# One left residual on ScalarE's DMA queue, and the third segment's main rows stored straight from SBUF

## The chip, the cores and the metric

The kernel runs on one core of a Trainium2 chip. The metric is the device time of one execution in microseconds (us), as a median of several runs. Before the change it is 1885.16 us (three runs, 1883.83 to 1887.8). The profiled execution has a span of 1876.8 us, at a mean granted TensorE clock of 0.993.

## What is computed

The result is `x + A(xn) + B(xn)` for one sequence of 2048 tokens of 1024 features, with `xn` the layer norm of `x`. B is a two-layer feed-forward net with a GELU. A is a recurrence over 64 segments of 32 tokens, each with 8 memory rows in front:

```python
def _A_ref(x, mem0, Wq, Wk, Wv, Wo, seg_len):
    ...
    mem = mem0
    for s in range(n_seg):                       # 64 segments of 32 tokens
        h = jnp.concatenate([mem, xs], axis=1)   # 8 memory rows and 32 tokens
        q = jnp.einsum('btd,dhe->bhte', h, Wq)   # k, v likewise; 32 heads of 128
        ...
        o = jnp.einsum('bhte,hed->btd', o, Wo)
        mem = o[:, :M, :].copy()                 # the next segment's memory
        outs.append(o[:, M:, :])

x = A_x
xn = _layernorm(x, axis=-1)
return x + _A_ref(xn, A_mem0, ...) + _B_ref(xn, B_w1, B_b1, B_w2, B_b2)
```

All tensors are bf16. A segment needs the memory rows of the one before, so the 64 segments run one after the other.

## The kernel before, in words

**First stage (to about 435 us).** Layer norm and the feed-forward net. `R_n` in DRAM gets `x + B(xn)`, the residual that A's rows are added to. `turn_R` (L426) copies its rows in DRAM into `hr_d` and `hrL_d`, where a later load finds them in the layout that the attention's output has. For the last 16 segments (the last four calls of `turn_R`) these copies aren't issued at once: they are put on a list, `small`, in segments s = 1 to 4 (L686), 13 or so in a segment, and are issued on GpSimd's queue one or two at a time, whenever a streamed weight unit is done (L672 to L674).

**Second stage: one pass per segment, for s = 0 to 63.** The weights Q, K, V and O are cut into 64 units of 128 x 2048 elements (512 KB), in the order K0, Q0, K1, Q1, V0, V1 (8 units each), O (16 units). 46 units stay in SBUF, 18 are streamed in each segment: two of these are copied from PSUM by VectorE, and the other 16 are loaded from DRAM on SyncE's queue into six rotating buffers. `start_stream` (L243) issues the next load in program order, when the unit that sat in the buffer has been used by TensorE.

Each segment's tokens are split. Its first 24 tokens and the 8 memory rows are the **main** rows, done in the segment itself. The last 8 tokens of four neighbouring segments are the **left** rows, done together as a group of 32 rows: `i4 = s % 4` says where in its group a segment is. Left rows go through O in segments with i4 = 1 (`left_o`), which therefore have two residuals to add: `st["res"]` for the main rows, in `res_home` (the right half of `hr_home`), and `st["resL"]` for the left rows, in `pr_all` (the last 256 columns of `half_home`). `pr_all` also holds the exponentials of the scores (L820), so `resL` can be loaded only when VectorE has read the last of them in this segment (L860), and the next segment's exponentials can be written only when the left rows have been stored.

**At the end of a segment**, in program order:

1. L975 loads the next segment's rows into `hr_home` (`load_x_rows`, L263): on ScalarE's queue for s < 5, on GpSimd's from s = 5 on. From s = 5 on that load brings the residual as well, so it overwrites `res_home` and must wait until the stores from it have landed. For s < 5 the residual comes by a load of its own on ScalarE's queue (L968, `load_res`).
2. In the loop over the O units (L992), `load_res` comes after unit 0, `resL` (L1000, i4 = 1) after unit 1, and in segments with i4 = 3 the closure `rows_of_main` after unit 2.
3. ScalarE casts the memory rows (L1005), TensorE multiplies them into place (L286) and VectorE copies them into the next segment's input (L290). Only then can the next segment's K0 pass begin.
4. VectorE adds the residuals to the accumulator in PSUM (L1020), `resL` first. The accumulator is one of three banks that rotate through all passes, and is free only after that.
5. The rows are stored. With i4 = 1 they go to a DRAM buffer `outL_d` by four stores (L1025) and from there to the output (L1050, by way of `small`). With i4 = 0 or 3, four stores of 24 x 512 bytes go from SBUF to the output (L1058). With i4 = 2, one store of 128 x 512 bytes goes to the DRAM buffer `outM_d` (L1052), and in the next segment SyncE copies it from there to the output, DRAM to DRAM (L1055).

Everything an engine does or issues is in one order, the program's. A wait on GpSimd's queue holds up all that stands behind it there.

Of the kernel before, what the change touches and what calls it, by code (L numbers as in the profile page):

```python
# [10 lines left out]
BF16 = mybir.dt.bfloat16  # L11
# [6 lines left out]
P = 128  # L18
# [19 lines left out]
NX = 24  # L38
NL = SEG - NX
GRP = 4  # L40
NGRP = NSEG // GRP
# [45 lines left out]
def kernel(  # L87
# [16 lines left out]
    nc = tc.nc  # L104
# [3 lines left out]
    out_flat = out.rearrange("b s d -> (b s) d")  # L108
# [10 lines left out]
    dram = ctx.enter_context(tc.tile_pool(name="dram", bufs=1, space=bass.MemoryType.DRAM))  # L119
# [3 lines left out]
    hrL_d = dram.tile([NGRP + 1, P, 512], BF16, name="hrL_d")  # L123
    R_n = dram.tile([S, DM], BF16, name="R_n")
    outL_d = dram.tile([NGRP, 2 * SEG, DM], BF16, name="outL_d")
    outM_d = dram.tile([NGRP, P, 256], BF16, name="outM_d")


    place = nc.lookup_mloc("DynamicDMAScratchLoc")
# [22 lines left out]
    def slab(place):  # L152
        if place in low:
            return low[place]
        return slabs.tile([P, 2048], BF16, name="u", tag=place)
# [10 lines left out]
    for j in range(4):  # L166
# [11 lines left out]
        out=m, in_=m, pattern=[[1, NX]], compare_op=ALU.is_ge, fill=0.0, base=0, channel_multiplier=-1,  # L178
    )
    for half in range(2):  # L180
        m = mask_left[0:SEG, :, 8 - 8 * half:16 - 8 * half]
        nc.gpsimd.affine_select(
            out=m, in_=m, pattern=[[-8, GRP], [0, 8]], compare_op=ALU.is_ge, fill=0.0, base=0, channel_multiplier=1,
        )
        nc.gpsimd.affine_select(
            out=m, in_=m, pattern=[[8, GRP], [1 if half else 0, 8]], compare_op=ALU.is_ge, fill=0.0,
# [110 lines left out]
    with tc.tile_pool(name="ma", bufs=2) as ma, tc.tile_pool(name="mps", bufs=6, space=PSUM) as mps:  # L297
# [35 lines left out]
        for j in range(4):  # L333
            nc.sync.dma_start(
                out=o_sb[32 * j + NX:32 * j + 32, 0:8, :],
                in_=mem0[:, 256 * j:256 * j + 256].rearrange("m (h e) -> m h e", h=8),
# [4 lines left out]
        for i in range(14):  # L341
            t = slab(f"w2_{i}")[:, :].rearrange("p (c d) -> p c d", d=DM)
# [146 lines left out]
        for tg in range(4):  # L489
# [14 lines left out]
            for fb in range(FC):  # L504
                ps = mps.tile([P, 512], F32, name="ps")
                for kt in range(KT):
# [9 lines left out]
                    out=xb[:, :], in_=ps[:, :], func=ACT.Identity, bias=b1col[:, fb:fb + 1], scale=1.0  # L516
# [4 lines left out]
                    out=u[:, :], in0=u[:, :], scalar1=0.044715, scalar2=1.0, op0=ALU.mult, op1=ALU.add  # L521
# [94 lines left out]
    with tc.tile_pool(name="late", bufs=1) as late, \  # L616
# [10 lines left out]
        def new_acc():  # L627
            bank = free_banks.popleft()
            ps = banks.tile([P, 512], F32, name="acc", tag=bank)
            bank_of[id(ps)] = bank, ps  # L630
            return ps
# [20 lines left out]
        def unit_tile(unit):  # L652
            nonlocal used
            if IS_STREAMED[unit]:
                used += 1
                return stream_tiles.pop(used - 1)[:, :]
            return res_tiles[unit]
# [8 lines left out]
        def unit_done(unit):  # L666

            if IS_STREAMED[unit]:
                start_stream(slot_of.pop(used - 1))
                if late_units:  # L670
                    fetch_late(late_units.popleft())
                for _ in range(2 if len(small) > 8 else 1):  # L672
                    if small:
                        small.popleft()()  # L674
# [7 lines left out]
        for s in range(NSEG):  # L682
            g, i4 = divmod(s, GRP)
# [12 lines left out]
            og, slot = divmod(s + 2, GRP)  # L696
            m0 = main_row(slot)
            st = {}
# [81 lines left out]
            def q_left(u):  # L780

                if i4 >= 2 + u and more:
                    q = qS[:, i4 - 2 - u, :, :]
                else:
                    q = qL[u][:, :, NL * i4:NL * i4 + NL]
                nc.vector.tensor_copy(out=q_home[:, :, 0:NL], in_=q)
# [13 lines left out]
            def scores(u, meanwhile=None):  # L800

                kT, qL_ends = st["kT", u], ends(q_home)
                sA = mixed[:, 0:160].rearrange("p (c q) -> p c q", q=40)
                sB = mixed[:, 160:224].rearrange("p (c q) -> p c q", q=16)
                for c in range(4):
                    for j in range(4):
                        q = slice(32 * j, 32 * j + 32)
                        nc.tensor.matmul(  # L808
                            sA[q, c, :], lhsT=kT[:, 4 * c + j, :], rhs=q_home[:, 4 * c + j, :],
                            start=(c == 0), stop=True, skip_group_check=True, tile_position=(0, 32 * j),  # L810
                        )
                    for j in range(4):
                        q = slice(32 * j, 32 * j + 32)
                        nc.tensor.matmul(  # L814
                            sB[q, c, :].rearrange("p (a b) -> p a b", b=NL), lhsT=kL[u][:, 4 * c + j, :],
                            rhs=qL_ends[:, 4 * c + j, :, :],
                            start=False, stop=True, skip_group_check=True, tile_position=(0, 32 * j),
                        )
                pr = pr_all[:, 0:224]
                nc.scalar.activation(out=pr, in_=mixed[:, 0:224], func=ACT.Exp, scale=INV_SQRT_DH)  # L820
                prA = pr[:, 0:160].rearrange("p (c q) -> p c q", q=40)
                prB = pr[:, 160:224].rearrange("p (c q) -> p c q", q=16)
                if meanwhile is not None:
                    meanwhile()
                for p, m in ((prA[:, :, NL:SEG], mask_order), (prB, mask_left[:, i4, :])):
                    n = m.shape[-1]
                    nc.vector.tensor_tensor(out=p, in0=p, in1=m[:, None, :].to_broadcast([P, 4, n]), op=ALU.min)
                st["pr", u] = prA, prB
# [94 lines left out]
            at = {} if first else {1: [lambda: q_left(0)]}  # L923
# [7 lines left out]
            if left_q[0] and not first:  # L931
# [4 lines left out]
            at = {  # L936
                0: [lambda: scores(0, None if first else lambda: q_left(1)), lambda: nc.vector.transpose(out=nat_home, in_=nat_home)],
                6: [lambda: sums(0)],
            }
# [19 lines left out]
            at = {0: [lambda: scores(1)], 4: [lambda: sums(1)]}  # L959
# [22 lines left out]
            if left_v[1]:  # L982
                at = {4: [lambda: values(1, (0,))], 6: [lambda: values(1, (1,))]}
            else:
                at = {5: [lambda: values(1, (0, 1))]}
            if left_v[1] and not first:
                at[9] = [lambda: left_values(1, psV1L)]
            at.setdefault(0, []).append(load_res)
            if i4 == 3:
                at.setdefault(2, []).append(rows_of_main)  # L990
            psX = new_acc()
            for n, unit in enumerate(O_UNITS):  # L992
                t = unit_tile(unit)
                o_product(unit, t, psX)
                unit_done(unit)
                for fn in at.get(n, ()):
                    fn()
                if n == 1 and left_o:
                    st["resL"] = pr_all
                    nc.gpsimd.dma_start(out=st["resL"][:, :], in_=hrL_d[og, :, 256:512])  # L1000
            nw = 2 if left_o else 1
            if not final:
                o_sb = nat_home
# [13 lines left out]
            res, rows = st["res"], slice(s * SEG, s * SEG + NX)  # L1017
# [13 lines left out]
            if final:  # L1031
                engines = [nc.sync, nc.scalar, nc.gpsimd]
                n = 0
                for w, r in enumerate(tiles):
                    for b in range(2):
                        cs = slice(256 * (2 * b + w), 256 * (2 * b + w) + 256)
                        pieces = [(rows, slice(64 * b + m0, 64 * b + m0 + NX))]
                        for sl, row in left_rows:
                            p0 = 64 * b + NL * sl
                            pieces.append((slice(row, row + NL), slice(p0, p0 + NL)))  # L1040
                        for o, i in pieces:
                            engines[n % 3].dma_start(out=out_flat[o, cs], in_=r[i, :])
                            n += 1
            elif left_o:
                pairs = [(out_flat[rows, :], outL_d[og, m0:m0 + NX, :])]
                pairs += [
                    (out_flat[row:row + NL, :], outL_d[og, NL * sl:NL * sl + NL, :]) for sl, row in left_rows
                ]
                for o, r in pairs:
                    small.append(lambda o=o, r=r: nc.gpsimd.dma_start(out=o, in_=r))  # L1050
            elif i4 == 2:
                nc.gpsimd.dma_start(out=outM_d[g, :, :], in_=res[:, :])  # L1052
                o = out_flat[rows, :].rearrange("t (j c) -> j t c", j=4)
                r = outM_d[g, :, :].rearrange("(j t) c -> j t c", j=4)[:, 0:NX, :]
                rows_of_main = lambda o=o, r=r: nc.sync.dma_start(out=o, in_=r)  # L1055
            else:
                for j in range(4):
                    nc.gpsimd.dma_start(out=out_flat[rows, 256 * j:256 * j + 256], in_=res[32 * j:32 * j + NX, :])  # L1058
# [37 lines left out]
```

## Time and profile before

| what | value |
|---|---|
| median of 3 runs | 1885.16 us |
| span of the profiled execution | 1876.8 us |
| TensorE busy | 1724.5 us (92%) |
| VectorE, ScalarE, GpSimd busy | 903.2, 650.0, 233.3 us |
| DMA | 614.17 MB, mean 327 GB/s |
| first segment's L1005 | at 458.6 us |
| last segment's L1005 (s = 62) | at 1848.0 us |

A segment is measured here from one L1005 (the cast of its memory rows) to the next. By that measure the 62 segments s = 1 to 62 take 22.4 us each on average. In a view by windows, "PEclk" is the granted share of TensorE's clock, and "DMA share" the time that packets took, as a share of the 16 DMA engines' time; 1.00 is a full set of engines. In a list of waits the three numbers are the sum in us, how often, and the longest. In a timeline, what stands in brackets is how long the engine was idle before an instruction, and what ended that; "issue" means that the trace shows no semaphore which ended it.

### The profile page before, as it was taken

To read this page: it belongs to the slowest core of one execution; us is meant where nothing else is said; L and a number is where in the kernel's file an instruction comes from. 1 tells how busy PE (TensorE), PEld (TensorE's weight loads), DVE (VectorE), ACT (ScalarE), POOL (GpSimd) and SP (SyncE) were. 2 spreads that over 40 slices of the span, in tenths; PEclk is the share of its full clock that TensorE was granted. 3 is DMA by queue.
4 is the path that set the end of the run, shared out by engine and by line. 5 is a ranking of instruction groups with operands and counts; after the bars stand their busy time and mean duration, and the time that the engine had idled before them with its cause. 6 is when DMAs were issued, how large, how long until landed. Compare 5 with 4: busy or idle time off the path is not lost.

```text
span 1876.8 us, 72814 instructions
## 1 busy us (share of the span) xinstructions
PE 1724.5 (92%) x32228; PEld 933.2 (50%) x32228; DVE 903.2 (48%) x2190; ACT 650.0 (35%) x1384; POOL 233.3 (12%) x464
## 2 busy tenths in 40 slices
PE   7999999998799998999999999999999889999887
PEld 3444444444355545555555555455555454555444
DVE  6657483704344444444444444444444444444443
ACT  5434252502233333333333333333333333333333
POOL 0000000000341111111111110101111111111111
PEclk9999999999899999999999999999999999999999
DMA  9821211499899999999999999999999999999998
GB/s 334 268 56 47 54 49 49 143 356 350 316 391 404 378 388 385 382 381 381 380 392 373 394 383 405 388 381 396 380 385 379 372 375 376 381 388 386 381 372 313
DMA packets 219672, 614.17 MB, mean 327 GB/s; under 512 B 45547, under 2 KB 65435, under 8 KB 219356
## 3 DMA queue, kind: packets, MB, share of 16 engines
q1 hardware_dynamic: 200892, 590.16, 82.9%
q0 software_dynamic: 14368, 16.71, 2.7%
q8 instruction: 252, 4.13, 0.9%
q10 hardware_dynamic: 4096, 2.64, 0.5%
q14 instruction: 64, 0.52, 0.1%
HBM read 595.19 MB, written 30.28 MB: 333 GB/s over the span
## 4 chain that ended last, share of the span: by engine, by line
PE 44%; DMA 19%; DVE 4%; issue 3%; ACT 2%; POOL 0%; DVEq 0%; ACTq 0%; POOLq 0%; SPq 0%
PE acc L706 30%; DMA u<-Wc_K 10%; PE acc L903 9%; DMA u<-Wc_O 4%; DMA outL_d<-half_home 2%; PE acc L875 2%; DMA u<-Wc_V 2%; ACT mixed L849 1%; DMA u<-Wc_Q 1%; DVE b_oL L764 1%; PE mixed L808 1%; DVE pd_main L856 1%; DVE u L241 1%; ACT mixed L846 1%; PE mixed L814 1%
## 5 line engine op out<-in xcount | busy, mean ns | idle before, releaser
L706 PE MATMUL acc<-u,hr_home 128*32 128x512 bf16 x11520 | 784.6, 382 | 42.5 <-issue 11.9
L706 PEld LDWEIGHTS <-hr_home 128*32 128x32 bf16 x12288 | 349.2, 97 | 333.1 <-issue 70.5
L706 PE MATMUL acc<-u,hrL 128*32 128x512 bf16 x2880 | 259.0, 379 | 9.8 <-issue 5.3
L903 PE MATMUL acc<-u,d_oL 128*32 128x256 bf16 (+1 forms) x3552 | 179.5, 291 | 24.8 <-issue 11.9
L507 PE MATMUL ps<-u 128*128 128x512 bf16 x896 | 196.3, 382 | 2.6 <-ACT u L391 2.6
L241 DVE TENSOR_SCALAR u<-kept 128x512 uint32<-128x512 uint32 x254 | 163.5, 686 | 34.8 <-PE acc L903 11.3
L903 PEld LDWEIGHTS <-b_oL 128*32 128x32 bf16 x3569 | 111.9, 98 | 71.0 <-issue 38.9
L556 PE MATMUL ps<-u 128*128 128x512 bf16 x672 | 147.0, 379 | 0.0
L903 PEld LDWEIGHTS <-d_oL 128*32 128x32 bf16 (+1 forms) x3552 | 103.7, 98 | 78.6 <-issue 37.2
L507 PEld LDWEIGHTS <-u 128*128 128x128 bf16 x896 | 88.2, 98 | 109.5 <-issue 4.6
L856 DVE TENSOR_TENSOR pd_main<-half_home,mixed 128x320 bf16<-128x320 bf16 x128 | 62.5, 488 | 153.1 <-ACT mixed L849 149.8
L903 PE MATMUL acc<-u,b_oL 128*32 128x256 bf16 (+1 forms) x1618 | 107.4, 290 | 17.8 <-DMA u<-Wc_O 9.0
L764 DVE STREAM_TRANSPOSE b_oL<-b_oL 128x512 bf16<-128x512 bf16 x128 | 90.7, 708 | 65.4 <-ACT b_oL L750 65.4
L706 PEld LDWEIGHTS <-hrL 128*32 128x32 bf16 x3072 | 90.4, 96 | 59.5 <-issue 21.6
L903 PE MATMUL acc<-W_O,b_oL 128*32 128x256 bf16 (+1 forms) x1776 | 109.3, 289 | 5.4 <-issue 5.2
L750 ACT CAST kT<-acc 128x512 bf16<-128x512 f32 x64 | 37.4, 585 | 219.2 <-PE acc L706 219.2
L263 POOL DMA_DIRECT2D hr_home<-hr_d x58 | 32.2, 556 | 610.5 <-PE acc L706 604.7
L750 ACT CAST b_oL<-acc 128x512 bf16<-128x512 f32 x128 | 75.2, 587 | 93.4 <-PE acc L706 93.4
L556 PEld LDWEIGHTS <-u 128*128 128x128 bf16 x672 | 65.3, 98 | 77.4 <-DVE g_u L523 0.4
L1005 ACT CAST d_oL<-acc 128x256 bf16<-128x256 f32 (+1 forms) x63 | 26.9, 426 | 213.4 <-PE acc L903 213.4
L515 ACT ACTIVATE g_xb<-ps,b1col 128x512 bf16<-128x512 f32 x112 | 76.8, 686 | 61.3 <-PE ps L507 60.2
L849 ACT ACTIVATE mixed<-mixed,small_consts 128x160 f32<-128x160 f32 x256 | 94.2, 368 | 8.4
(124 smaller groups left out, 1941.8 us busy)
## 6 DMA issues: line engine op xcount, KB each, us to landing
u<-Wc_K SPq DMA_DIRECT2D x320, 512.0 KB
u<-Wc_V SPq DMA_DIRECT2D x256, 512.0 KB
u<-Wc_O SPq DMA_DIRECT2D x256, 512.0 KB
u<-Wc_Q SPq DMA_DIRECT2D x128, 512.0 KB
u<-Wc_O SPq DMA_DIRECT2D x64, 320.0 KB
hr_home<-hr_d POOLq DMA_DIRECT2D x58, 128.0 KB, 5.4
u<-in_B_w_dram SPq DMA_DIRECT2D x14, 512.0 KB
u<-in_A_Wq_dram SPq DMA_DIRECT2D x14, 512.0 KB
```

The source lines that it names most:

```text
L241: nc.vector.tensor_single_scalar(out=out, in_=in_, scalar=0, op=ALU.bitwise_or)
L263: eng.dma_start(out=hr_home[:, 0:n], in_=hr_d[s, :, 0:n])
L507: nc.tensor.matmul(ps[:, :].rearrange("p (s t) -> p s t", t=SEG), lhsT=w1_sb[fb // 14 * 8 + kt][:, (fb % 14) * P:(fb % 14 + 1) * P], rhs=x ...
L515: nc.scalar.activation(out=xb[:, :], in_=ps[:, :], func=ACT.Identity, bias=b1col[:, fb:fb + 1], scale=1.0)
L556: nc.tensor.matmul(ps[:, :], lhsT=gts[fc // 4][:, fc % 4, t * P:(t + 1) * P], rhs=w2_sb[fc // 2][:, fc % 2, cs], start=(fc == 0), stop=(fc ...
L706: nc.tensor.matmul(o, lhsT=lhs[:, i, :], rhs=m, start=(i == seq[0]), stop=(i == seq[-1]), tile_position=(0, 32 * j),)
L750: cp(out=out, in_=ps.rearrange("p (h e) -> p h e", e=32))
L764: nc.vector.transpose(out=home, in_=home)
L849: nc.scalar.activation(out=mixed[:, 160 * b:160 * b + 160], in_=mixed[:, 0:160], func=ACT.Exp, scale=-1.0, bias=off[:, b:b + 1],)
L856: nc.vector.tensor_tensor(out=pdA.rearrange("p c b q -> p b c q"), in0=prA[:, None, :, :].to_broadcast([P, 2, 4, 40]), in1=dd, op=ALU.mult,)
L875: nc.tensor.matmul(oV[r][:, c, :, :], lhsT=V[q, c * P:(c + 1) * P], rhs=pdA[q, c, :, :], start=(c == 0), stop=False, skip_group_check=True ...
L903: nc.tensor.matmul(acc[r:r + n // 8, c:c + wide], lhsT=lhs[:, 4 * (i % 4) + 2 * u + k, :], rhs=w_t[:, c0 + c:c0 + c + wide], start=(unit = ...
```

## The change

Two edits that don't touch each other:

- In segment s = 1 the left residual `resL` is loaded on ScalarE's queue. In the other segments with i4 = 1, and in the last one, it stays on GpSimd's.
- In segments with i4 = 2 (16 of them) the main rows are stored as in those with i4 = 0 and 3: four stores on GpSimd's queue straight from `res_home` to the output. The DRAM buffer `outM_d`, the store to it and SyncE's copy out of it are gone.

It is for freeing GpSimd's queue of one load early in the second stage, and for taking the detour through DRAM out of the data's path.

```diff
-    outM_d = dram.tile([NGRP, P, 256], BF16, name="outM_d")
...
             at.setdefault(0, []).append(load_res)
-            if i4 == 3:
-                at.setdefault(2, []).append(rows_of_main)
...
                     st["resL"] = pr_all
-                    nc.gpsimd.dma_start(out=st["resL"][:, :], in_=hrL_d[og, :, 256:512])
+                    (nc.scalar if s < 5 else nc.gpsimd).dma_start(
+                        out=st["resL"][:, :], in_=hrL_d[og, :, 256:512]
+                    )
...
-            elif i4 == 2:
-                nc.gpsimd.dma_start(out=outM_d[g, :, :], in_=res[:, :])
-                o = out_flat[rows, :].rearrange("t (j c) -> j t c", j=4)
-                r = outM_d[g, :, :].rearrange("(j t) c -> j t c", j=4)[:, 0:NX, :]
-                rows_of_main = lambda o=o, r=r: nc.sync.dma_start(out=o, in_=r)
             else:
                 for j in range(4):
                     nc.gpsimd.dma_start(out=out_flat[rows, 256 * j:256 * j + 256], in_=res[32 * j:32 * j + NX, :])
```

## The prediction

> **What bounds the kernel now.** I read the page first, then a table of windows by segment, the list of waits, and the timelines of GpSimd, VectorE and TensorE around what stood out.
>
> The windows of s = 1 to 4:
>
> ```profile
> 458.60:480.30 21.70, 20.24 (x398) 10.34 (x400) 10.40 (x25) 7.26 (x17) 7.58 (x14) 1.00 1.02 397
> ```
> ```profile
> 481.78:512.49 30.71, 21.10 (x487) 11.41 (x486) 10.60 (x26) 7.47 (x17) 11.46 (x21) 0.83 0.75 270
> 512.49:535.05 22.56, 21.03 (x510) 12.35 (x506) 10.09 (x24) 7.80 (x19) 7.81 (x14) 1.00 1.01 393
> 535.05:558.07 23.02, 21.00 (x511) 12.44 (x506) 10.29 (x24) 7.80 (x18) 10.48 (x19) 1.00 1.01 391
> ```
>
> The last three figures are TensorE's clock, the DMA share and GB/s. The DMA share is about 1.0 in every segment but one, with some 390 GB/s: **the weight stream bounds the second stage**, TensorE (19 to 21 us busy of 22) comes next. So only what stops the DMA engines, or gives them less to move, moves the end. The exception is s = 2, at 30.71 us against a mean of 21.28 us in the other segments with i4 = 2. The waits name it:
>
> ```profile
> DVE half_home L1020 <- DMA half_home<-hrL_d: 9.3, 1, 9.3
> ...
> PE acc L706 <- DVE hr_home L1020: 8.1, 1, 8.1
> ```
>
> It happens once in 64 segments. The load of `resL` in s = 1 comes late, and GpSimd's timeline tells why:
>
> ```profile
> 475.67 1.11 POOL L455 DMA_DIRECT2D hr_d<-R_n  x2 [3.70 <-issue]
> 476.76 0.55 POOL L455 DMA_DIRECT2D hrL_d<-R_n  x1
> 481.91 1.12 POOL L455 DMA_DIRECT2D hr_d<-R_n  x2 [4.60 <-issue]
> 483.02 0.55 POOL L455 DMA_DIRECT2D hrL_d<-R_n  x1
> 488.52 0.57 POOL L1000 DMA_DIRECT2D half_home<-hrL_d  x1 [4.96 <-issue]
> 493.06 1.11 POOL L1025 DMA_DIRECT2D outL_d<-half_home  x2 [3.96 <-DVE half_home L1020]
> ```
>
> The load stands behind 13 copies of residual rows, and GpSimd pauses 4 to 5 us after every few of them although nothing that they need is missing. Each pause ends about 0.35 us after an older transfer of this queue lands (488.17 before the issue at 488.52). I read that as a queue with little room. If a transfer takes one place for each 16 rows of 512 bytes, plus one, 22 places fit (my estimate); stepping through the queue with that and 5.6 us to landing gives the 488.52 as 487.0, the 518.63 of `outM_d`'s first store as 518.4, the 565.52 of the stores of s = 4 as 566.7.
>
> **What the skill says.** "DMA: Bandwidth & Descriptors", section "SWDGE vs HWDGE vs iDMA": GpSimd writes its DMAs' descriptors into rings in SBUF, and transfers issued from ScalarE don't use those. The pauses fit this, and ScalarE's loads show none. Its section "Issuing engines are not separate DMA queues": another issuing engine saves only issue time, the bytes share 16 engines. The landings agree: 5.2 us from GpSimd, and 6 to 7.5 us for ScalarE's loads that VectorE waited for in s = 2. "TensorE: Matmul & The Clock Gate", section "Part 1: The HAM clock gate": after about 3.4 us idle the clock halves. Here TensorE stops at 485.07 and the clock is at half from 488.39 to 498.63, 3.3 us later and for 10.24 us.
>
> **Edit 1, the load.** It removes one GpSimd issue (0.57 us) and adds one on ScalarE (0.33 to 0.77 us, the two L968 of s = 1 and 2). VectorE's last read of `pr_all` ends at 474.95, so it is issued at 475 to 475.7. Behind it on ScalarE is the cast of V's product at 477.33: not held up. Landing is bounded by 5.2 us and 7.5 us; I take 6.8: 482.2, bounds 480.3 to 483.2. VectorE reaches L1020 at 482.99. The wait is gone, and TensorE's 8.06 us with it.
>
> Its price is counted in DMA time. In windows of 1 us the DMA share stays at 0.94 or more until 488, then is 0.78, 0.49, 0.10, 0.04, 0.00, 0.00, 0.27, 0.20, 0.51, 0.98, 0.61 and 0.90 up to 500: 7.1 us are missing. The segment's share of 0.75 gives 0.25 x 30.71 = 7.7. I take **7.5 us** (9.4 is the bound by the segment's length).
>
> **What is queued on GpSimd gives part of it back.** The copies of s = 1 to 4 go at the pace of landings, not of TensorE. Stepping the same queue with TensorE 7.5 us earlier leaves it where it was (within 0.5 us). Four things then meet it:
>
> - s = 1: the second half of the left rows' store, issued at 493.6 now, finds no room until 488.5, lands at about 494, and holds the exponentials (due about 490.3). TensorE can be held some 3 us.
> - s = 3 and 4: `load_res` must wait until the stores of the segment before have landed, at 524.3 and 548.4; with the shift it would be issued at 523.1 and 546.0. The residual is late by about 2 us. The K0 pass runs meanwhile on another bank, so I cost both at nothing.
> - s = 5: the load of the next rows (L263) is GpSimd's and must wait for the stores of s = 4:
>
> ```profile
> 565.52 2.10 POOL L1058 DMA_DIRECT2D out_dram<-hr_home  x4 [2.31 <-DVE qL L750]
> 573.45 0.57 POOL L263 DMA_DIRECT2D hr_home<-hr_d  x1 [5.83 <-DMA u<-Wc_O]
> ```
>
> The fourth store is issued at 567.12 and lands 5.3 us later, at 572.46. Now TensorE asks for the load only at about 573.4, so this wait is hidden. With the shift TensorE asks at 566, the stores still land at 572.5 to 574.5, the load is issued at about 573.3, lands 5.3 us later, and L290 (581.49 now, 574.0 shifted) runs at about 579. **TensorE idles about 5 us.** The weight queue covers the first 3.7 us, as it did after 485.07. The other 1.3 us are lost, and the half clock, which then lasts some 8 us: before, 493 to 498.6 at half clock cost 3.3 us of DMA share, which I take again. Give-back: 1.3 + 3.3 = 4.6, rounded to **4 us**, since part of the shift is spent at s = 3 and 4. The hold in s = 2 is within the 3.7 us. From s = 6 on GpSimd has no backlog.
>
> **Edit 2, the stores.** Rows of the DMA view (KB each, landing):
>
> ```profile
> outM_d<-hr_home POOLq DMA_DIRECT2D x16, 64.0 KB, 5.1
> ...
> out_dram<-outM_d SPq DMA_DIRECT2D x16, 48.0 KB
> ```
>
> Per group it removes one store (0.56 us issue) and SyncE's copy (0.64 us), and adds four stores of 12 KB (0.51 us each): GpSimd 1.5 us more, behind which stands only the next segment's load, some 14 us later. In packets: the store is 16 of 4096 bytes at 159 ns, one an engine. The copy is 96 of 512 bytes at 27 ns, 24 on each of four engines: its semaphore rises by twelve at once and then four times by one. That is how "Why a DMA increments its semaphore by 16 and not by 1", on the same DMA page, has an outer dimension of 4 run on four engines. The four stores are 48 of 1024 bytes at 46 ns, twelve engines with four each. With 9 ns a completion an engine has, on average, 168 + 162 = 330 ns before and 138 + 36 = 174 ns after. Saved: 0.156 us x 16 = **2.5 us** of the bound resource. If the four engines of the copy set the pace, (648 + 168 - 220) ns x 16 = 9.5 us. But the 16 engines' landings of one weight load spread over 2.2 us, no more after that copy than elsewhere, so I don't expect it. If the twelve engines do, 52 ns x 16 = 0.8 us are lost. SyncE's 0.64 us cost nothing: its loads stand 6.4 us ahead of their landing.
>
> **Sum.** 1885.2 - 7.5 + 4.0 - 2.5 = **1879.2 us**.
>
> **The rivals.**
>
> - *The whole stall is recovered.* GpSimd's backlog shrinks with the load's wait, and L263 comes when TensorE asks. For it: the load waited 4 us there, and VectorE's wait held the next stores. Against: that the queue was at its room's pace before and after. 1885.2 - 7.5 - 2.5 = 1875.2.
> - *The stall moves whole.* A second half-clock period in s = 2 or a later landing in s = 5 costs what was gained; the packets bring 1 us. 1884.2.
> - *Slower.* Two stalls for one, not covered by queued weights: 3.5 and 5 us, each with 3.3 us of half clock, are 15.1 us. 1885.2 - 7.5 + 15.1 - 1 = 1891.8. For it: the four stores take 12 places where one took 9, in s = 2, when places are short. Against: 3.7 us of cover were there at 485.
>
> **How the numbers follow.** Forecast 0.55, whole recovery 0.18, moved whole 0.16, slower 0.11. The bound of 0.2% is 3.8 us: faster is below 1881.4. Of the forecast 0.48 lies there, with recovery 0.18 and 0.02 of the third: 0.68. Slower (above 1888.9) 0.10. The same 0.22. The range is 1874.0 to 1886.5: it takes in the recovery and the third rival, and leaves out the slower one and an edit 2 worth much more than 2.5 us.
>
> **What would show it.** Right: in s = 1 no wait of L1020 for `half_home`; s = 2 takes 21 to 24 us; s = 5's L290 waits for `hr_home<-hr_d`, a new entry of some 5 us, with a new half-clock period near 580; the span from s = 6 on shorter by 2 to 3 us. Wrong: s = 5 unchanged at 20.4 us (recovery), ScalarE waiting several us before its load, or segments with i4 = 3 that get longer.

## The result, and the profile after

| | us |
|---|---|
| predicted | 1879.2 (1874.0 to 1886.5) |
| before, 4 runs | 1884.63 (1883.83 to 1887.8) |
| after, 4 runs | 1871.57 (1867.91 to 1873.48) |
| ratio | 0.9925, 95% interval 0.9904 to 0.9947 |

The kernel became faster, as forecast, but by more: the ratio is 0.0075 x 1884.6 = 14.1 us (10.0 to 18.1), and 6.0 us had been forecast. A second measurement of the same pair on another chip (both_again, below) gave 0.9947 (0.9926 to 0.9968), which is 10.0 us (6.0 to 13.9). So 6 us lies outside the first interval and at the lower edge of the second.

**How far one trace can be trusted here.** Single executions of the kernel before ran from 1868.4 to 1893.9 us in 62 runs on one chip. The traces show where: by L1005 (see above), the way from s = 12 to s = 62, where edit 1 changes nothing, took 1113.0 us before, 1113.2 after and 1118.5 in both_again. Spans of single traces therefore decide nothing below 10 us. What is read from them below is local: the way from s = 0 to s = 6, where GpSimd's backlog lies. The whole kernel is compared by medians and ratios of many runs.

**The profile after.** The windows of s = 1 to 6, by segment as before (line numbers are one to six lower now: L1019 is L1020 of before, L289 was L290, L262 was L263, L1052 was L1058, L997 was L1000; the other runs' lines are shifted by a few likewise). After its length a window gives the busy time of TensorE's matmuls, of its weight loads, of VectorE, ScalarE and GpSimd, then the clock, the DMA share and GB/s:

```profile
459.23:482.61 23.38, 21.53 (x413) 11.54 (x417) 10.40 (x25) 7.26 (x17) 9.28 (x17) 1.00 1.01 393
482.61:503.12 20.51, 18.67 (x487) 10.58 (x487) 10.74 (x26) 7.46 (x17) 7.61 (x14) 1.00 1.03 404
503.12:525.76 22.64, 20.98 (x511) 12.56 (x507) 10.09 (x24) 7.81 (x18) 9.35 (x17) 1.00 1.02 400
525.76:549.33 23.57, 21.20 (x510) 12.37 (x506) 10.20 (x24) 7.81 (x18) 10.39 (x19) 1.00 0.99 368
549.33:572.39 23.06, 21.77 (x413) 11.61 (x409) 10.41 (x25) 7.28 (x17) 8.24 (x16) 1.00 1.03 405
572.39:594.41 22.02, 19.11 (x486) 10.62 (x485) 10.76 (x26) 7.55 (x17) 5.21 (x10) 1.00 0.99 375
```

The second line is s = 2: 20.51 us where it was 30.71, clock 1.00 and DMA share 1.03 where they were 0.83 and 0.75. The last is s = 6: 22.02 us, where it was 20.36. ScalarE's and VectorE's timelines have the left residual itself:

```profile
476.11 0.47 ACTq L997 DMA_DIRECT2D half_home<-hrL_d  x1
```
```profile
484.03 0.42 DVE L1019 TENSOR_TENSOR half_home<-acc,half_home 128x256 bf16<-128x256 f32 x1 [0.20 <-DMA half_home<-hrL_d]
```

It is issued at 476.11 and comes 0.20 us late, where it came 9.34 us late. It lands at 483.90, 7.8 us after the start of its issue, where 6.8 had been taken and 7.5 was the upper bound. In load_only it took 8.2 us and in both_again 9.2, and VectorE waited 0.67 and 0.94 us for it. Over the nine runs that have this edit and leave SyncE's queue without the copies of `small`, it took 6.3 to 9.2 us, and VectorE waited at most 1.81. GpSimd's timeline at the stores of s = 4 and the load for s = 6, then VectorE's and TensorE's at what waits for it:

```profile
560.85 2.11 POOL L1052 DMA_DIRECT2D out_dram<-hr_home  x4 [2.19 <-DVE pd_left L859]
568.68 0.56 POOL L262 DMA_DIRECT2D hr_home<-hr_d  x1 [5.72 <-DMA u<-Wc_O]
```
```profile
574.48 0.22 DVE L289 CAST hr_home<-mixed 128x64 bf16<-128x64 f32 x1 [4.25 <-DMA hr_home<-hr_d]
```
```profile
573.03 0.27 PE L285 MATMUL mixed<-ident_mem,d_oL 128*32 128x16 bf16 x16
573.14 0.82 PE L705 MATMUL acc<-u,hrL 128*32 128x512 bf16 x12
574.75 0.61 PE L705 MATMUL acc<-u,hr_home 128*32 128x512 bf16 x8 [0.79 <-DVE hr_home L289]
```

This is the give-back that was predicted, in its small form. Two of the releasers in brackets aren't the ones that ended the wait. VectorE had finished the sum of these rows at 550.82; the stores went out 0.31 us after an older copy of this queue had landed at 560.54, as in the pauses marked "issue". And TensorE had last read `hr_home` at 564.86; the load waits for the stores of s = 4: the last is issued at 562.45 and lands at 567.96, the load follows at 568.68 and lands at 574.38, and L289 waits for it and no longer for TensorE. But of VectorE's 4.25 us of idle time only the last is the load's doing: TensorE's product for L289 ends at 573.30, and it has units of the left rows to do meanwhile. Its gap is 0.79 us, not 5, and its clock isn't halved there.

### The profile page after: what moved, and what is told of

Its sections match the earlier page's. It is cut to its first block, busy times and chain, and to the rows that moved or that the text cites. A ratio compares the mean times of both kernels' runs of the same rounds, so it can differ in the third digit from the quotient of the medians.

```text
span 1866.2 us, 72871 instructions
## 1 busy us (share of the span) xinstructions
PE 1726.3 (93%) x32208; PEld 938.2 (50%) x32228; DVE 904.3 (48%) x2190; ACT 650.4 (35%) x1384; POOL 257.7 (14%) x511
## 4 chain that ended last, share of the span: by engine, by line
PE 65%; DMA 21%; DVE 5%; issue 4%; ACT 3%; POOL 1%; DVEq 0%; ACTq 0%; POOLq 0%; SPq 0%
PE acc L705 30%; PE ps L506 10%; DMA u<-Wc_K 10%; PE acc L902 9%; PE ps L555 8%; DMA u<-Wc_O 4%; DMA outL_d<-half_home 2%; DMA u<-Wc_Q 2%; PE ps L591 2%; ACT mixed L848 2%; PE acc L874 2%; DVE b_oL L763 1%; PE mixed L807 1%; DVE pd_main L855 1%; ACT mixed L845 1%
## 5 line engine op out<-in xcount | busy, mean ns | idle before, releaser
L705 PEld LDWEIGHTS <-hr_home 128*32 128x32 bf16 x12288 | 353.4, 97 | 318.1 <-issue 64.5
L902 PEld LDWEIGHTS <-b_oL 128*32 128x32 bf16 x3569 | 112.7, 99 | 67.8 <-issue 35.3
L1052 POOL DMA_DIRECT2D out_dram<-hr_home x188 | 96.6, 515 | 308.8 <-DVE hr_home L1019 296.2
L262 POOL DMA_DIRECT2D hr_home<-hr_d x58 | 32.4, 558 | 585.1 <-PE acc L705 566.4
```

The lines of the kernel that those rows point to most:

```text
L705: nc.tensor.matmul(o, lhsT=lhs[:, i, :], rhs=m, start=(i == seq[0]), stop=(i == seq[-1]), tile_position=(0, 32 * j),)
L902: nc.tensor.matmul(acc[r:r + n // 8, c:c + wide], lhsT=lhs[:, 4 * (i % 4) + 2 * u + k, :], rhs=w_t[:, c0 + c:c0 + c + wide], start=(unit = ...
```

## The experiments

Each runs against the kernel before on its own chip. "Faster by" is (1 - ratio) x the median of before, with the interval of the ratio. In the expectations, theory A is that the stall is recovered nearly whole, B that it is partly given back and edit 2 is worth more, C that the edits need each other.

**The single edits, both, and the detour three times.** load_only is the first of these on the kernel before, store_only the rest of the change:

```diff
-                    nc.gpsimd.dma_start(out=st["resL"][:, :], in_=hrL_d[og, :, 256:512])
+                    (nc.scalar if s < 5 else nc.gpsimd).dma_start(
+                        out=st["resL"][:, :], in_=hrL_d[og, :, 256:512]
+                    )
```

detour_three is load_only with these lines:

```diff
-    outM_d = dram.tile([NGRP, P, 256], BF16, name="outM_d")
+    outM_d = dram.tile([NSEG, P, 256], BF16, name="outM_d")
...
-            if i4 == 3:
+            if i4 != 2 and not first:
                 at.setdefault(2, []).append(rows_of_main)
...
-            elif i4 == 2:
-                nc.gpsimd.dma_start(out=outM_d[g, :, :], in_=res[:, :])
+            else:
+                nc.gpsimd.dma_start(out=outM_d[s, :, :], in_=res[:, :])
```

load_only: 

> Edit 1 alone: resL of s = 1 on ScalarE's queue, third segments still by way of outM_d. Theory A (the stall is recovered whole, since GpSimd's backlog moved forward with it: in the changed kernel the stores of s = 4 landed at 568.0 us, not at 572.5 to 574.5): 7 to 9 us less than before, and L290 of s = 5 costs TensorE under 1 us. Theory B (part is given back at s = 5, as predicted, and edit 2 is worth more than predicted): 3 to 4 us less, with a TensorE gap of 4 to 5 us near 575 us. Theory C (the two edits need each other: without the direct stores of s = 2 GpSimd's queue is late): 3 to 4 us less, with the stores of s = 4 landing at 572 us or later.

store_only: 

> Edit 2 alone: main rows of third segments straight to the output, resL of s = 1 still behind GpSimd's copies. Theory A: the stall of 8 us in s = 1 stays, and the packets saved bring 2.5 to 5 us. Theory B (the four DMA engines of SyncE's copy set the pace): 9 to 10 us less. Theory C: 2.5 us less, and the sum of the two single edits is clearly under the 13 us of both.

both_again: 

> The changed kernel once more, on the same chip as the single edits: 13 us less than before (10 to 18 by the first measurement). All theories expect that; it is the measure for whether the two single edits add up.

detour_three: 

> Edit 1, and the detour through DRAM in all segments without left rows: 48 stores to the buffer and 47 copies of SyncE, where the kernel before has 16 and 16. Its distance to load_only is twice edit 2, with the sign turned. By mean packets (0.156 us each): 5 us slower than load_only. By four engines that set the pace (0.6 us each): 19 us slower. If edit 2 is worth nothing by itself: the same as load_only.

| | median | ratio (interval) | faster by | s = 0 to 6 in the trace |
|---|---|---|---|---|
| before | 1881.83 (62 runs) | | | 142.2 |
| load_only | 1875.62 (22) | 0.9966 (0.9952 to 0.9981) | 6.4 (3.6 to 9.0) | 134.9 |
| store_only | 1878.42 (22) | 0.9990 (0.9970 to 1.0009) | 1.9 (-1.7 to 5.6) | 140.3 |
| both_again | 1874.97 (9) | 0.9947 (0.9926 to 0.9968) | 10.0 (6.0 to 13.9) | 137.1 |
| detour_three | 1877.45 (22) | 0.9972 (0.9955 to 0.9990) | 5.3 (1.9 to 8.5) | 137.7 |

(The 142.2 is from the trace shown in the prediction.) The single edits add up to 8.3 us, within the interval of both together, and in load_only the stores of s = 4 landed at 569.5 us, where C had 572 or later: C falls. B wanted 9 to 10 us from edit 2 alone, which has at most 5.6, so B falls too. detour_three made the detour 47 times where load_only makes it 16 times. It costs 1.1 us more by the ratios and 1.8 by the medians, with an interval of -2.1 to 6.7 (an estimate from the 22 runs of each). Four engines that set the pace would have cost 19; 5 us, and nothing, are both possible. In store_only the stall is there again, and in load_only it is gone. From the list of waits of store_only:

```profile
DVE half_home L1017 <- DMA half_home<-hrL_d: 7.2, 1, 7.2
PE acc L705 <- DVE hr_home L1017: 6.0, 1, 6.0
```

In load_only it is the gap at s = 6 again, from TensorE's timeline:

```profile
575.75 0.61 PE L706 MATMUL acc<-u,hr_home 128*32 128x512 bf16 x8 [0.88 <-DVE hr_home L290]
```

In both_again the gap is 2.19 us. The stores of s = 4 landed at 569.5 in load_only, 566.5 in both_again, 568.0 after: all before the 572.5 to 574.5 that I had worked out. In store_only, with the stall, they landed at 571.0. The other predicted hold, that of the exponentials of s = 2, shows as a gap of TensorE before the sums: 0.35 us after, 1.36 in both_again, 1.35 in load_only, 2.14 in detour_three, where I had some 3.

**Is it the backlog? The copies on another queue.** copies_on_sync is the kernel before, both_sync the changed kernel, with

```diff
-                        small.append(lambda o=o, r=r: nc.gpsimd.dma_start(out=o, in_=r))
+                        small.append(lambda o=o, r=r: nc.sync.dma_start(out=o, in_=r))
```

copies_on_sync: 

> The kernel before, with one thing changed: the residual copies of s = 1 to 4 (the list small, lines L455) are issued on SyncE's queue instead of GpSimd's. resL stays on GpSimd's queue, the detour stays. If the stall of s = 1 comes from the backlog on GpSimd's queue: resL is issued at about 475 to 476 us, TensorE's gap of 6 to 8 us at s = 2 is gone, s = 2 takes 21 to 22.5 us, and the time is that of load_only, 6 us less than before. If the load were late for another reason (its own landing under a full weight stream, or what it waits for): the gap stays. SyncE's queue gets 57 issues of 0.6 us more, which may cost 1 to 2 us.

both_sync: 

> Both edits, and the copies of s = 1 to 4 on SyncE's queue: a try for a better version. It takes away what is left of the give-back: no gap of 1 to 2 us before the matmuls that wait for the exponentials of s = 2, none of 0.8 to 2.2 us at the start of s = 6. Expected 1 to 3 us less than both_again if the give-back is real, the same or slower if SyncE's extra issues hold up the weights.

Measured: 1897.76 us, ratio 1.0090 (1.0057 to 1.0124), 17 us slower than before; both_sync 1898.34, ratio 1.0076 (1.0051 to 1.0102). The stall of s = 1 is gone, though `resL` stayed on GpSimd's queue: issued at 478.55, when VectorE had read the last of `pr_all`, with no gap of TensorE of over 1.5 us before s = 2. But the copies now hold up the weights. Windows of s = 1 to 4 in copies_on_sync:

```profile
459.98:486.70 26.72, 22.52 (x413) 11.69 (x417) 10.31 (x25) 7.33 (x17) 2.58 (x5) 1.00 0.90 312
486.70:514.71 28.01, 20.54 (x487) 11.99 (x487) 10.66 (x26) 7.55 (x17) 3.68 (x7) 0.94 0.92 318
514.71:540.83 26.12, 22.68 (x509) 12.94 (x505) 10.14 (x24) 7.81 (x18) 0.58 (x1) 0.93 0.91 317
540.83:572.20 31.37, 23.24 (x508) 13.66 (x504) 10.29 (x24) 7.77 (x19) 2.07 (x4) 0.86 0.91 309
```

All four segments are long, and the DMA share is 0.91 in place of 1.0, at 315 GB/s in place of 390: the engines are in part idle, and move less in the time that they are busy. From s = 0 to 6 it takes 157.7 us, 22.8 more than load_only, for 57 copies: 0.40 us each. Against before_spread (below), the nearer comparison, it is 24.8 us, 0.43 each. The experiment answered the question on the stall, and my 1 to 2 us for its side effect was wrong by more than a factor of ten.

**The same question without the side effect: the copies thinly.** before_spread is the kernel before, both_spread the changed one, with

```diff
-            if 1 <= s <= 4:
-                turn_R(NT - 5 + s, small)
+            if s > 6 and i4 in (3, 0):
+                k = 2 * ((s - 7) // 4) + (s - 7) % 4
+                if k < 16:
+                    turn_R(NT - 4 + k // 4, small, (k % 4,))
```

where the last argument of `turn_R` picks one of its four segments.

before_spread: 

> The kernel before, with one thing changed: the residual copies of s = 1 to 4 stay on GpSimd's queue, but come later and thinly, those of one segment (3 to 6 copies) in each of s = 7, 8, 11, 12 and so on up to 36. resL of s = 1 stays on GpSimd's queue. If the stall of s = 1 is the backlog of that queue: resL is issued at about 475 to 476 us, no gap of TensorE before s = 2, the time from the L1005 of s = 0 to that of s = 6 is 133 to 136 us (142.2 and 140.3 with the stall), and the whole is 7 to 9 us less than before, without edit 1. If resL is late for another reason: 140 to 142 us, and no gain.

both_spread: 

> Both edits, with the same thin copies: a try for a better version. It takes away the hold of 1.4 us before the exponentials of s = 2 and the gap of 0.8 to 2.2 us at s = 6, which are what is left of the give-back: the time from s = 0 to s = 6 is 133 to 135 us, where both_again and the changed kernel have 137.1 and 135.2, and the whole is 1 to 2 us less than both_again. If the copies hold up GpSimd's loads in the later segments: 1 to 3 us more.

Measured: before_spread 1872.52 us, ratio 0.9948 (0.9930 to 0.9966), 9.8 us faster than before (1881.21 there), **with neither of the two edits**. both_spread 1873.08, ratio 0.9949 (0.9930 to 0.9969). From s = 0 to 6 they take 132.9 and 131.5 us. GpSimd's timeline of before_spread:

```profile
473.13 0.56 POOL L1002 DMA_DIRECT2D half_home<-hrL_d  x1 [12.54 <-issue]
480.81 1.12 POOL L1027 DMA_DIRECT2D outL_d<-half_home  x2 [7.12 <-DVE hr_home L1022]
```

No copy stands before the load, and it goes out when `pr_all` is free. The stall was the backlog of GpSimd's queue and nothing else in that load: taking the queue's other work away does what taking the load off the queue does. It may do a little more, since in its trace s = 2 and s = 6 are free of holds as well, but its 9.8 us (6.4 to 13.2) overlap load_only's 6.4 (3.6 to 9.0), so that isn't shown. As a version, both_spread can't be told from both_again: 0.9949 against 0.9947, though from s = 0 to 6 it is 5.6 us shorter in the trace.

**How much is given back, as a function of the backlog's end.** Both have the changed kernel's edits, and in s = 4 more copies of residual rows that are there already (segment 44's three, or the 13 of segments 44 to 47):

```diff
             if 1 <= s <= 4:
                 turn_R(NT - 5 + s, small)
+            if s == 4:
+                turn_R(NT - 5, small, (0,))          # later_thirteen: range(4)
```

later_three: 

> Both edits, and three more residual copies on GpSimd's queue in s = 4 (those of one segment, with the values that are there already): the backlog ends one turn of the queue later, and the stores of s = 4 land at about 572 to 574 us instead of 566.5 to 568, which is what the prediction had. By the prediction's own step: the load of s = 5 is issued 5 us later, TensorE idles 5 us more at the start of s = 6, with a half-clock period, and the time is 3 to 4 us over both_again. If the weight queue and the units that TensorE does ahead cover more than was thought: a gap under 3 us, and under 1 us of time.

later_thirteen: 

> As later_three, but with the copies of four segments more (13): the stores of s = 4 land some 20 us later than in both_again, at 587 to 590 us, and the load of s = 5 with them. If that load is what gives time back, TensorE idles 17 to 21 us at the start of s = 6, with a half-clock period, and the time is 15 to 20 us over both_again. If TensorE isn't held by it: the same time as both_again.

GpSimd's and TensorE's timelines of later_three:

```profile
567.76 1.00 POOL L1054 DMA_DIRECT2D out_dram<-hr_home  x2 [2.96 <-issue]
573.50 0.57 POOL L262 DMA_DIRECT2D hr_home<-hr_d  x1 [4.74 <-DMA u<-Wc_K]
```
```profile
576.70 1.04 PE L707 MATMUL acc<-u,hr_home 128*32 128x512 bf16 x8 [4.41 <-DVE hr_home L289]
```

Here the stores of s = 4 land at 572.54, the very time the prediction had, and what it had for that time happens: a gap of 4.41 us (5 predicted), a clock at half from 575.7 for 6.8 us, and 142.0 us from s = 0 to 6 where both_again has 137.1, not all of it from here. In s = 6 alone it takes 26.98 us, where the changed kernel and both_again have 22.0 and 23.3: 3.7 to 5.0 us more, and 4 had been predicted for this case. The whole kernel took 1877.61 us, ratio 0.9983 (0.9963 to 1.0003), 2.6 us over both_again by the medians and 6.8 by the ratios, on different chips. In later_thirteen the gap is 12.12 us, s = 0 to 6 takes 148.8 us, and the whole 1884.26, ratio 1.0007 (0.9989 to 1.0026): no gain is left that can be told from zero. I had expected the stores at 587 to 590 us. They landed at 579.3: with TensorE stopped the weight stream stopped too (47 GB/s from 576 to 583 us), the stores landed 1.6 to 1.7 us after their issue, and the queue ran faster.

**Does the copy's use of few DMA engines set the pace?** Both are load_only with eight more of SyncE's copies in each segment with i4 = 3, into a buffer of their own:

```diff
                 at.setdefault(2, []).append(rows_of_main)
+                for n, fn in enumerate(again):
+                    at.setdefault(3 + n, []).append(fn)
...
+                again = [
+                    lambda o=again_d[g, n, :, :, :], r=r: nc.sync.dma_start(out=o, in_=r)
+                    for n in range(8)
+                ]                    # nine_on_twelve: o and r with "j t c -> t j c"
```

nine_on_four: 

> Edit 1 with the detour, and SyncE's copy of third segments done nine times: eight more copies of 48 KB into another DRAM buffer, one after each of the O units 3 to 10 of segments with i4 = 3 (128 more in all). Outer dimension 4, so each runs on four DMA engines. If a copy costs what its 96 packets are of 16 engines (0.16 us): 21 us more than load_only. If the four engines set the pace (24 packets of 27 ns, 0.65 us): 83 us more, with segments of i4 = 3 at 27 to 28 us in place of 22.5. If it is the issue on SyncE's queue (0.64 us each, not hidden): also about 80 us.

nine_on_twelve: 

> As nine_on_four, with the outer dimensions of the eight extra copies exchanged (24 outside, 4 inside), so that each runs on twelve DMA engines with 8 packets on each. By mean packets: 21 us more than load_only, as nine_on_four. If the engines in use set the pace: 0.22 us each, 28 us more, and 55 us less than nine_on_four. If the issue on SyncE's queue sets it: the same 80 us as nine_on_four.

Measured: nine_on_four 1915.66 us, ratio 1.0184 (1.0149 to 1.0219); nine_on_twelve 1925.28, ratio 1.0233 (1.0193 to 1.0274). Against load_only that is (1.0184 - 0.9966) x 1881 = 41 us and 50 us for 128 copies, 0.32 and 0.39 us each. The pair isn't as clean as I meant it: with the outer dimension of 4, each of the extra copies went out as four runs of 12288 bytes, not as 96 of 512, so the two differ in packets too. Such a packet took 0.46 us (median). So for nine_on_four the four engines would cost 59 us and the packets' mean 15 us; for nine_on_twelve it is 28 and 21 us as expected. Neither account fits both: if the engines in use set the pace, nine_on_twelve costs half of nine_on_four, and it cost no less; the packets' mean is too small twice. What all three experiments with bunched copies on SyncE's queue agree on is the size, 0.3 to 0.45 us a copy, for copies of 8 to 64 KB. Whether that is SyncE's issue time (medians of 0.55 us and 0.74 us each here) less what the queued weights cover, or something between the copies and the weights on the DMA engines, stays open.

## Why the prediction was right and wrong, point by point

- **What bounds the kernel, and the stall.** Right. That `resL` was late because of the backlog on GpSimd's queue is shown from two sides: by load_only, which moves the load, and by before_spread, which moves the backlog.
- **Edit 1, the load on ScalarE's queue.** Right in what it does: the wait of 9.34 us is down to 0.20, at most 1.81 in any run with this edit, and ScalarE wasn't held up (0.47 us). The landing was past its upper bound, 7.8 us after the issue instead of 6.8; TensorE had work meanwhile.
- **What the queue gives back.** The chain is right, link by link: the load of s = 5 waits for the stores of s = 4, L290 waits for the load, TensorE for L290. So is the view of s = 3 and 4: VectorE waited up to 1.8 us for the late residual in the changed kernel, and TensorE had no gap over 1 us there. The step that failed is "leaves it where it was (within 0.5 us)", and with it the term "at 572.5 to 574.5" for the landing of those stores. They landed at 568.0, 4.5 us earlier than before. GpSimd's timelines show where that comes from. The first copy of s = 2, before:

```profile
498.81 1.16 POOL L455 DMA_DIRECT2D hr_d<-R_n  x2
```

The last copy ahead of the place where `resL` stood, and the first copy of s = 2, after:

```profile
480.70 0.55 POOL L454 DMA_DIRECT2D hrL_d<-R_n  x1
494.40 1.16 POOL L454 DMA_DIRECT2D hr_d<-R_n  x2
```

| us on GpSimd's queue, from issue to issue | before | store_only | after | load_only | both_again |
|---|---|---|---|---|---|
| first store of s = 0 to last copy ahead of `resL` | 21.3 | 19.1 | 18.9 | 18.8 | 19.6 |
| from there to the first copy of s = 2 | 15.8 | 16.6 | 13.7 | 13.9 | 14.5 |
| from there to the first store of s = 4 | 66.7 | 65.9 | 66.5 | 67.2 | 67.8 |

In the first stretch neither edit acts. In its one execution before was some 2 us longer there, its transfers taking 5.9 us from issue to landing, against 5.2 to 5.5 in the other four: that is chance. In the second stretch lay `resL`, with VectorE's wait behind it. Without them it is 1.3 to 2.9 us shorter, which the stepping had at nothing. In the third the pace is the same, as predicted. I had stepped through all of it with 5.6 us to landing, fitted to the issue times of that one execution; over the third stretch the transfers took 5.3 us before and after. At 568 the gap is 0.8 to 2.2 us, not 5, and no half clock follows it. later_three, which puts the landing at 572.5, shows that the rest of the step was sized about rightly.

- **So the first rival came nearest**, and its reason, that the backlog shrinks with the load and its wait, holds for about half of the 4.5 us. The other half is luck: with the slow start that the execution read had, the stores would have landed some 2 us later. What is still given back is small and not sharply known: s = 6 takes 22.0, 23.3 and 21.8 us in the changed kernel, both_again and load_only, 20.4 and 21.1 in before and store_only, and 21.4 in both kernels with thin copies.
- **Edit 2.** 2.5 us was forecast. store_only has 1.9 (-1.7 to 5.6), and both_again less load_only 3.6 by the ratios, 0.7 by the medians; none of these differs from 2.5 or from zero. detour_three less load_only is about twice edit 2, so it gives 0.9 us (-1.1 to 3.5). The 9.5 us of "the four engines set the pace" are ruled out. The 0.8 us of loss are not, so no gain from edit 2 is shown.
- **The sum.** With the give-back at some 1 us (an estimate from the gap of 0.8 us) instead of 4 it would have been 1885.2 - 7.5 + 1 - 2.5 = 1876.2, which is 9 us less than before. That is inside the second interval (6.0 to 13.9) and just short of the first (10.0 to 18.1). The rest of the distance to 1871.6 isn't explained by a mechanism: the second measurement of the same pair has 1874.97, before was 1881.8 there, and the median of so few runs moves by some us in a kernel whose executions differ by 25. How much of the 9 us is the stall's 7.5 and how much edit 2's 2.5 isn't settled either: load_only, which has edit 1 with its give-back, gained 6.4 (3.6 to 9.0).

## What to carry to other kernels

A transfer's lateness is often that of what stands before it in its queue: moving the load and thinning the queue were both a cure here. Removing a stall brings forward what TensorE asks for, and a queue at its own pace only by what its own waits took in the stall, so step through that queue with the landing times of the trace. Read the start of a long backlog from more than one execution: here chance moved its end by 2 us. Small transfers that looked free by their packets cost 0.3 to 0.45 us each here when they stood bunched in the queue that carries the bounding stream.

## What the runs showed of the hardware that I hadn't expected

- Every period at half clock that lies between 460 and 1840 us in these traces is 3.41 us long or two, three or four times that. After a gap of TensorE of 8.06 us it was 10.24 us, after 4.41 us 6.83, after 12.12 us 13.65. A gap of 2.19 us in both_again had none, and yet the short periods come without a long gap: later_three has one of 3.41 us from 500.62 us on, and the longest gap there is 1.96 us. So half a clock doesn't need the 3.4 us of idle time that the prediction names.
- 64 KB issued from ScalarE under the full weight stream landed 7.8, 8.2 and 9.2 us after the start of its issue (changed kernel, load_only, both_again). Transfers from GpSimd took 5.3 us on average in the same stretch, and 1.6 to 1.7 us when TensorE stood still (later_thirteen).
- 57 copies of 8 to 64 KB from DRAM to DRAM: with them spread thinly on GpSimd's queue the kernel takes 1872.52 us (before_spread), with them on SyncE's queue among the weights 1897.76 (copies_on_sync).
